# The first expert's threshold search: eight of fourteen rounds behind a branch

## The chip, the core and the metric

The kernel runs on one core of a Trainium2 chip. Its engines are TensorE (PE, matmuls; PEld are its weight loads), VectorE (DVE), ScalarE (ACT), GpSimd (POOL) and SyncE (SP, which here issues DMAs); each works off its own queue of instructions in order, and they wait for each other by semaphores. The metric is the device time of one execution in microseconds.

## What is computed

Attention over blocks, and behind it a mixture of eight experts whose tokens are chosen greedily. Cut to what matters:

```python
def _moe_ref(x, w_gate, w1, w2):        # x: 4608 tokens x 512, from the attention
    logits = x @ w_gate                 # 4608 x 8
    order = np.argsort(-logits.flatten())
    for idx in order:                   # best (token, expert) pairs first
        tok, e = idx // 8, idx % 8
        if assigned[tok] >= 0 or counts[e] >= 576: continue
        assigned[tok] = e; counts[e] += 1
    for e in range(8):
        out[assigned == e] = np.maximum(x[assigned == e] @ w1[e], 0) @ w2[e]
```

The kernel does not sort. It asks which expert is filled first: each token proposes its best open expert, and the expert whose 576th proposal is the highest takes its 576 tokens. Then tokens and expert are struck out and the same is done for the next.

## The kernel before

Up to about 315 us the attention runs; its last step gives the logits `L`. The second stage routes and computes eight experts. `route(k)` finds expert k and its tokens, `gather` fetches them by an indirect DMA of GpSimd, `weights` fetches the expert's weights by SyncE and splits them into two fp16 halves, and `ffn` does the two matmuls (`h`, then `y`). For k from 1 on `route` runs beside the `ffn` of an earlier expert. For k = 0 nothing runs beside it: there are no tokens yet.

`route` holds the proposals twice, as `PV` (a token's logits on one partition) and as `PB` (transposed, so that each group of partitions holds one expert). The search finds the 576th proposal of all experts at once. Each of `NS` = 14 rounds cuts the interval to a quarter: it places three borders in it (`cd`, `bs`), counts the proposals above each (two counts `jk` on VectorE, line 761 or 762, one count `ja` on ScalarE, line 735, by an accumulated sign), sums the counts over partitions by a small matmul (`tot`, line 782), and derives by how many quarters the lower border `lo` moves (`sg`, line 785). At round `NSC` = 6 the proposals are shifted by the border reached (`P2`, line 739), so that the later, smaller steps keep their precision.

After the last round lines 789 to 827 choose: two additions and three small transposes bring border and width to every partition (`th`, `bc`), a maximum finds the expert, and a one-hot vector `oh` picks its borders (`los`, `lo2s`, `hi2s`) and its number `ei`. From these come a mask of the tokens above the interval (`MM[:,0]`) and of those at or above the lower border (`ge`); the difference is `MM[:,1]`, of which as many are taken as there is room for. `eidx` (line 824) is the expert's number, which SyncE loads into a register (line 926) before it fetches the weights. Scans (`SC`, line 831) and position matmuls (`po`, lines 843 to 850) number the tokens, `invert` makes the list `ix` (lines 884 to 913), eight matmuls `warm` (line 920) keep TensorE at work until the gather (`xg`, line 985) lands, and transposes (`xt`, line 1006) put the tokens in the layout of `h` (line 1040).

The order on the engines is made by a planner (`Sched`), when the program is built: the pieces are Python generators that yield engine and cost, and the planner takes the one that can start first. A queue holds instructions in the order in which it took them. `sc.busy`, `sc.lag` and the yielded costs are its estimates; what changes in them changes how later pieces are woven into each other.

Of the kernel before, what the change touches and what calls it, by code (L numbers as in the profile page):

```python
# [596 lines left out]
class Moe:  # L597
    def __init__(s,tc,nc,ctx,sc,L,xd,w1,w2,out):
        s.tc,s.nc,s.sc,s.L,s.xd,s.w1,s.w2,s.out=tc,nc,sc,L,xd,w1,w2,out
        s.NT=xd.shape[0]; s.D=w1.shape[1]; s.E=w1.shape[0]; s.F=w1.shape[2]; s.CAP=s.NT//s.E; s.C=s.NT//P  # L600
        s.NS=14; s.NSC=6
        s.cp=ctx.enter_context(tc.tile_pool(name="mcp",bufs=1))
        s.ident=s.cp.tile([P,P],F32,name="mident"); make_identity(nc,s.ident)
        s.am=s.cp.tile([P,8],F32,name="m_am"); s.nam=0; nc.gpsimd.memset(s.am,2.0**-50)
        s.ab=s.cp.tile([P,1],F32,name="m_ab")
        s.vm=s.cp.tile([P,s.C],F32,name="m_vm"); s.nP=s.cp.tile([P,s.C,s.E],F32,name="m_nP"); s.Lr=s.cp.tile([P,s.C,s.E],F32,name="m_Lr")
        N=s.C*s.E; s.PAD=s.CAP*s.E//P
        s.PB,s.P2=[s.cp.tile([P,N+s.PAD],F32,name=n) for n in ("m_PB","m_P2")]
# [86 lines left out]
    def route(s,k):  # L695
# [19 lines left out]
        else:  # L715
# [29 lines left out]
            for t in range(s.NS):  # L745
                w=4.0**-t
                cnt=rp.tile([P,3],F16,tag="cnt",name=f"cn{k}_{t}")
                cand=base
                if t:
                    cand=rp.tile([P,3],F32,tag="cand",name=f"cd{k}_{t}")  # L750
                    yield D,s.CD[0 if k==0 else 1 if k<3 else 2],('P2',k) if PBx is not PB else None
                    if k==0: V.tensor_tensor(cand[:,2:3],base[:,2:3],nw,op=OP.add)
                    else:
                        for i in (2,0,1): V.tensor_scalar(cand[:,i:i+1],lo,nw,(i+1)*w,op0=OP.add,op1=OP.add)
                P2=s.P2 if t==s.NSC else None
                sc.add(signs(PBx,cand[:,2:3],cnt,t,P2),s.PR['signs'],sc.now+200)
                sc.nolat()
                for i in range(2):
                    yield D,429
                    jk=rp.tile([P,N],F16,tag="jk",name=f"jk{k}_{t}_{i}")  # L760
                    if t and k==0: V.scalar_tensor_tensor(jk,base[:,i:i+1].to_broadcast([P,N]),nw,PBx[:,:N],op0=OP.add,op1=OP.is_gt,accum_out=cnt[:,i:i+1])  # L761
                    else: V.tensor_scalar(jk,PBx[:,:N],cand[:,i:i+1],0.0,op0=OP.is_lt,op1=OP.add,accum_out=cnt[:,i:i+1])
                    if i==0: sc.nolat()
                if k==0 and t==3:
                    dg=rp.tile([32,1024],F16,name="m_dg",bufs=1)
                    nc.gpsimd.indirect_dma_start(out=dg,out_offset=None,in_=s.xd,in_offset=bass.IndirectOffsetOnAxis(ap=s.it[:32,P-1:P],axis=0))
                add=lambda o,a,b: V.tensor_tensor(o,a,b,op=OP.add) if k==0 else V.tensor_scalar(o,a,b,None,op0=OP.add)
                if t: add(lo,lo,nw)
                if P2 is not None:
                    V.tensor_scalar(CB[:,2:3],lo,-1.0,None,op0=OP.mult); sc.set(('nlo',k))  # L770
                    lo=CB[:,1:2]; PBx=P2
                if t==s.NS-1: add(CB[:,2:3],CB[:,0:1],lo)
                elif k==0:
                    base=rp.tile([P,3],F32,tag="base",name=f"bs{k}_{t}")
                    V.tensor_scalar(base,s.io3g,w/4,lo,op0=OP.mult,op1=OP.add)
                    if t==1:
                        V.reciprocal(s.g[:,2:3],s.g[:,1:2])
                        nc.gpsimd.tensor_scalar(fl(Lm),fl(s.L),s.g[:,2:3],None,op0=OP.mult)
                sc.busy(D,330 if k==0 else 150)
                yield T,30,('sg',k,t)  # L780
                tot=s.ps.tile([P,512],F32,tag="tot",name=f"tot{k}_{t}")
                nc.tensor.matmul(tot[:,0:3],lhsT=s.bo,rhs=cnt,start=True,stop=True)  # L782
                yield D,72
                sg=rp.tile([P,4],F32,tag="sg",name=f"sg{k}_{t}")
                V.scalar_tensor_tensor(sg[:,0:3],tot[:,:3],s.NT-s.CAP+0.5,(wk[:,t:t+1]).to_broadcast([P,3]),op0=OP.is_le,op1=OP.mult,accum_out=sg[:,3:4])
                nw=sg[:,3:4]
                sc.lag(s.XG if k>2 and t<s.XT else s.LG)
            yield D,140
            V.tensor_scalar(CB[:,2:3],CB[:,2:3],nw,None,op0=OP.add)
            V.tensor_scalar(lo,lo,nw,None,op0=OP.add)  # L790
            yield T,90,'rt'
            tk=sc.take(); ps=s.ps.tile([P,512],F32,tag="rt",name=f"bc{k}")
            th=s.ps.tile([P,512],F32,tag="tot",name=f"th{k}")
            nc.tensor.transpose(th[:,:32],CB[:32,2:3].to_broadcast([32,P]),s.ident[:32,:32])
            for i in range(2): nc.tensor.transpose(ps[:,32*i:32*i+32],CB[:32,i:i+1].to_broadcast([32,P]),s.ident[:32,:32])
            BC=s.BC[k%2]; th=th[:,0:8]

            f=rp.tile([P,2,8],F32,tag="f",name=f"f{k}"); m1=rp.tile([P,6],F32,tag="m1",name=f"m1{k}")
            yield D,77
            V.tensor_reduce(m1[:,0:1],th,axis=AX.X,op=OP.max)  # L800
            yield D,138
            V.scalar_tensor_tensor(f[:,0],th,m1[:,0:1],s.wt8,op0=OP.is_equal,op1=OP.mult)
            V.tensor_copy(BC[:,0:2],ps[:,:64].rearrange("p (i x) -> p i x",i=2)[:,:,0:8])
            V.tensor_scalar(BC[:,2],ps[:,32:40],w if k else wk[:,s.NS-1:s.NS],None,op0=OP.add); sc.set(tk)
            yield D,77
            V.tensor_reduce(m1[:,1:2],f[:,0],axis=AX.X,op=OP.max)
            oh=f[:,1]
            yield D,133
            V.tensor_scalar(oh,f[:,0],m1[:,1:2],None,op0=OP.is_equal)
# [12 lines left out]
            ge=rp.tile([P,C],F16,tag="ge",name=f"ge{k}")
            V.tensor_scalar(ge,ds_,los,lo2s,op0=OP.subtract,op1=OP.is_ge)
            V.tensor_copy(eidx,ei)
            sc.add(s.weights(k,eidx),s.PR['weights'],sc.now)
            yield D,106
            V.tensor_tensor(MM[:,1],ge,MM[:,0],op=OP.subtract)
# [307 lines left out]
```

## Time and profile before

| | us |
|---|---|
| median of three runs | 765.41 |
| lowest, highest | 763.78, 765.56 |
| the profiled execution, time | 765.04 |
| the profiled execution, span from first to last instruction | 763.3 |
| busy in that span: TensorE, VectorE, ScalarE, GpSimd | 709.0, 561.3, 514.5, 380.5 |

The profile is of one execution. A row of the instructions in order of time gives the start and the duration in us, the engine, the line, the operation, and output <- input; in brackets stands how long the engine idled before and what ended it. Shares over the whole span say little here, since the two stages and the seam between them have different limits; rows of the seam, from 315 to 365 us, are what is read below.

### The profile page before, as it was taken

Reading aid. Unit: us, or ns where it says so; the run is one execution under the profiler, and the core shown is the slowest. Engines: PE = TensorE matmul, PEld = TensorE weight load, DVE = VectorE, ACT = ScalarE, POOL = GpSimd, SP = SyncE. Lnnn points to the kernel's source line nnn. Section 1 sums busy time; section 2 is a strip of 40 time slices with the busy share of each in tenths; the row PEclk is TensorE's granted clock in tenths of the full one; section 3 lists DMA queues with packets and bytes.
Section 4 is the critical chain, followed back from the end, with each engine's and each line's share of the span. In section 5 each row is a group of like instructions: output and inputs, shape, how many; then the busy total and the mean of one; then the engine's idle time right before and its main releaser. Section 6 shows DMA issues by size and latency. Waiting matters only on the chain.

```text
span 763.3 us, 18351 instructions
## 1 busy us (share of the span) xinstructions
PE 709.0 (93%) x6321; PEld 456.9 (60%) x6321; DVE 561.3 (74%) x2293; ACT 514.5 (67%) x1395; POOL 380.5 (50%) x455
## 2 busy tenths in 40 slices
PE   5999999999999999417999999999989999999997
PEld 3666776666666766305546747657556475574753
DVE  6999989798979979887989978869678596020210
ACT  4887889878787777335838778594964956583211
POOL 6876563636655652203414457293670843796001
PEclk9999999999999999856999999999999999999999
DMA  9899999999999998608027075591963916992001
GB/s 194 163 204 192 213 206 186 230 177 232 185 229 187 220 201 166 186 4 280 6 109 230 8 259 149 169 220 41 256 133 135 239 36 222 211 282 70 32 15 48
DMA packets 273517, 124.48 MB, mean 163 GB/s; under 512 B 247296, under 2 KB 256512, under 8 KB 273424
## 3 DMA queue, kind: packets, MB, share of 16 engines
q1 hardware_dynamic: 267504, 104.37, 63.2%
q0 software_dynamic: 5920, 18.95, 8.2%
q8 instruction: 49, 0.80, 0.5%
q14 instruction: 44, 0.36, 0.2%
HBM read 71.39 MB, written 18.87 MB: 118 GB/s over the span
## 4 chain that ended last, share of the span: by engine, by line
PE 49%; issue 4%; DMA 2%; DVE 2%; ACT 1%; POOL 1%; POOLq 0%; DVEq 0%; ACTq 0%
PE h L1040 25%; PE y L1066 19%; PE y L1070 3%; DMA raw<-in_moe_w_dram 1%; PE pe L901 1%; DMA xg<-x,ix 1%; DVE jk L761 1%; POOL xg L985 1%; PE xt L1006 0%; PE tot L782 0%; PE psb L487 0%; DMA out_dram<-yo,ix 0%; PE psb L437 0%; ACT ja L735 0%; POOL W L948 0%
## 5 line engine op out<-in xcount | busy, mean ns | idle before, releaser
L1040 PE MATMUL h<-X,W 128*128 128x320 f16 (+3 forms) x1536 | 195.2, 287 | 0.6 <-DVE HL L1028 0.5
L393 ACT ACTIVATE P<-psb,m 128x576 f32<-128x576 f32 (+8 forms) x288 | 149.6, 548 | 38.5 <-DVE m L389 35.4
L1040 PEld LDWEIGHTS <-W 128*128 128x128 f16 x1536 | 142.9, 98 | 42.5 <-issue 3.0
L948 POOL TENSOR_TENSOR W<-raw,W 128x1024 f16<-128x1024 f32 x56 | 118.4, 2137 | 80.2 <-ACT W L946 79.7
L1066 PE MATMUL y<-W,HH 128*128 128x512 f16 x512 | 152.4, 379 | 0.0
L385 DVE TENSOR_REDUCE m<-psb 128x1 f32<-128x576 f32 (+8 forms) x288 | 124.5, 479 | 11.4 <-PE psb L367 10.7
L437 PE MATMUL psb<-mident,P 128*128 128x128 f32 x800 | 105.6, 279 | 4.8 <-DVE Xf L454 1.7
L437 PEld LDWEIGHTS psb<-mident,P 128*128 128x128 f32 x800 | 85.8, 141 | 23.4 <-ACT P L393 6.6
L1026 ACT ACTIVATE HH<-h 128x320 f16<-128x320 f32 (+3 forms) x128 | 51.8, 411 | 68.9 <-PE h L1040 67.4
L1066 PE MATMUL y<-W,HL 128*128 128x512 f16 x256 | 97.1, 379 | 0.0
L487 PE MATMUL psb<-PT,V 128*64 128x448 f32 (+5 forms) x776 | 96.7, 390 | 0.2 <-ACT PT L418 0.2
L1056 POOL DMA_INDIRECT out_dram<-yo,ix x40 | 39.1, 977 | 114.3 <-ACT yo L1048 78.7
L367 PE MATMUL psb<-kT,qT 128*64 128x512 f16 (+7 forms) x640 | 86.6, 294 | 3.1 <-ACT P L393 1.3
L367 PEld LDWEIGHTS <-qT 128*64 128x64 f16 x1280 | 61.4, 111 | 38.8 <-issue 17.7
L418 ACT ACTIVATE PT<-psb 128x512 f32<-128x512 f32 (+1 forms) x157 | 79.3, 580 | 7.4 <-PE psb L437 5.5
L1028 DVE SCALAR_TENSOR_TENSOR HL<-h,HH 128x320 f16<-128x320 f32 (+3 forms) x128 | 57.3, 452 | 36.2 <-ACT HH L1026 35.7
L367 PE MATMUL psb<-kS,qT 128*64 128x512 f16 (+7 forms) x640 | 78.9, 289 | 0.0
L1066 PEld LDWEIGHTS <-HH 128*128 128x128 f16 x512 | 46.5, 98 | 53.3 <-issue 2.6
L942 ACT ACTIVATE raw<-raw 128x512 f32<-128x512 f32 x112 | 67.5, 625 | 11.2 <-DMA raw<-in_moe_w_dram 11.2
L487 PEld LDWEIGHTS psb<-PT,V 128*64 128x64 f32 x776 | 48.6, 138 | 34.9 <-issue 24.4
L946 ACT ACTIVATE W<-raw 128x512 f16<-128x512 f32 x112 | 67.7, 625 | 0.0
L393 ACT ACTIVATION_READ_ACCUMULATOR P<-psb,m 128x1 f32 x288 | 65.1, 226 | 0.0
(230 smaller groups left out, 1034.5 us busy)
## 6 DMA issues: line engine op xcount, KB each, us to landing
raw<-in_moe_w_dram SPq DMA_DIRECT2D x64, 512.0 KB, 5.7
x<-XR SPq DMA_DIRECT2D x8, 1152.0 KB, 6.9
kn<-in_k_dram SPq DMA_DIRECT2D x15, 576.0 KB, 6.1
qn<-in_q_dram SPq DMA_DIRECT2D x15, 576.0 KB, 8.1
V<-in_v_dram SPq DMA_DIRECT2D x64, 128.0 KB, 2.9
V<-in_v_dram SPq DMA_DIRECT2D x16, 64.0 KB, 2.9
xg<-x,ix POOLq DMA_INDIRECT x40, 4.6
out_dram<-yo,ix POOLq DMA_INDIRECT x40, 2.9
```

Source lines behind the costliest of these rows:

```text
L367: nc.tensor.matmul(ps[64 * h:64 * h + 64, o + a:o + e], lhsT=A[:, h, 64 * i:64 * i + 64], rhs=K[:, h, a:e], start=st, stop=not st)
L385: nc.vector.tensor_reduce(m[:, 0, c:c + 1], ps[:, o:o + 64 * (i + 1)], axis=AX.X, op=OP.max)
L393: nc.scalar.activation(Pt[:, s.OFF[i]:s.OFF[i] + 64 * (i + 1)], ps[:, o:o + 64 * (i + 1)], AF.Exp, bias=m[:, 1, c:c + 1], scale=s.ESC, acc ...
L418: s.nc.scalar.activation(out, in_, AF.Copy)
L437: nc.tensor.transpose(ps[:, a], s.Pb[n % s.NP][:, s.OFF[i] + 128 * j:s.OFF[i] + 128 * j + P], s.ident)
L487: nc.tensor.matmul(ps[64 * h:64 * h + 64, 64 * (i0 - b0):64 * (b1 - b0)], lhsT=vn[:, j, 2 * (n % 2) + h, :], rhs=pt[:, s.PTI[(j, i0)]:s.PT ...
L942: nc.scalar.activation(raw[:,x],raw[:,x],AF.Copy,scale=s.WS)
L946: nc.scalar.activation(hi[:,x],raw[:,x],AF.Copy)
L948: nc.gpsimd.tensor_tensor(lw,raw,hi,op=OP.subtract)
L1028: nc.vector.scalar_tensor_tensor(HL[:,f,ts],ps,0.0,HH[:,f,ts],op0=OP.max,op1=OP.subtract)
L1040: nc.tensor.matmul(ps,lhsT=W[:,a,d,f*P:f*P+P],rhs=X[:,4*(d//2)+d%2+l,ts],start=(d==0 and n==0),stop=(d==3 and n==2))
L1066: if m<4: nc.tensor.matmul(ps,lhsT=Z[:,f,m*P:m*P+P],rhs=Y[:,a,f],start=(f==n==0),stop=(f==7 and n==2))
```

## The change

Only the first search changes. It runs six rounds and chooses at once. A flag `bi` says whether that choice may stand: it is 0 if one expert alone has the highest border (the sum of `f` equals its maximum) and if exactly 576 of its logits are at or above the lower border (`cg`, summed by a matmul with ones). VectorE, TensorE and ScalarE load the flag into a register, and the block with rounds 7 to 14 and a second choice is jumped over when it is 0. `eidx` moves behind that block. The rounds and the choice become inner functions, and for the block they are built without the planner; behind it the planner is told that three engines were busy 1500 ns.

```diff
-        s.NS=14; s.NSC=6
+        s.NS=14; s.NSC=6; s.TB=6
...
-            for t in range(s.NS):
-                w=4.0**-t
...
+            def rounds(t0,t1):
+                nonlocal lo,nw,PBx,base
+                for t in range(t0,t1):
+                    w=s.wlast=4.0**-t
...
+                    if t<s.TB or k: sc.add(sg_,s.PR['signs'],sc.now+200)
+                    else:
+                        next(sg_); next(sg_,0)
...
+                    if t and (k or t!=s.TB): add(lo,lo,nw)
...
+            def choose(t1,n,guess):
...
+                V.scalar_tensor_tensor(f[:,0],th,m1[:,0:1],s.wt8,op0=OP.is_equal,op1=OP.mult,**(dict(accum_out=m1[:,6:7]) if guess else {}))
...
+                V.tensor_scalar(MM[:,0],ds_,los,hi2s,op0=OP.subtract,op1=OP.is_gt)
+                if guess:
+                    with nc.allow_low_precision(reason="whole numbers up to 36"):
+                        V.tensor_scalar(ge,ds_,los,lo2s,op0=OP.subtract,op1=OP.is_ge)
+                        V.tensor_reduce(cg[:,0:1],ge,axis=AX.X,op=OP.add)
+                else: V.tensor_scalar(ge,ds_,los,lo2s,op0=OP.subtract,op1=OP.is_ge)
+                if k: load()
+                yield D,106
+                V.tensor_tensor(MM[:,1],ge,MM[:,0],op=OP.subtract)
...
+            if k:
+                yield from rounds(0,s.NS)
+                yield D,140
+                end()
+                yield from choose(s.NS,1,False)
+            else:
...
+                yield from rounds(0,s.TB)
+                yield D,140
+                V.tensor_tensor(CB[:,2:3],lo,nw,op=OP.add)
+                V.tensor_tensor(lo,lo,nw,op=OP.add)
+                yield from choose(s.TB,1,True)
+                yield T,100
+                tot=s.ps.tile([P,512],F32,tag="tot",name="m_ct")
+                nc.tensor.matmul(tot[:,0:1],lhsT=s.ones,rhs=cg,start=True,stop=True)
+                yield D,150
+                V.tensor_tensor(bad[:,0:1],m1[:,6:7],m1[:,1:2],op=OP.not_equal)
+                V.scalar_tensor_tensor(bi,tot[:,0:1],float(s.CAP),bad[:,0:1],op0=OP.not_equal,op1=OP.max)
+                ET=mybir.EngineType
+                rv=nc.values_load(bi[0:1,0:1],engines=(ET.DVE,ET.PE,ET.Activation),min_val=0,max_val=1)
+                with s.tc.If(rv>0):
+                    for x in rounds(s.TB,s.NS): pass
+                    end()
+                    for x in choose(s.NS,0,False): pass
+                for x in (D,T,A): sc.busy(x,1500)
+                yield D,150
+                load()
```

VectorE's queue behind the sixth round's decision (`sg_5`), before: the next round follows, and far below `eidx` stands between the mask `ge` and its difference.

```order
L785 SCALAR_TENSOR_TENSOR sg_5_5040<-tot_5_5038,m_wkg 128x3
L752 TENSOR_TENSOR cd_6_5043<-bs_5_5036,sg_5_5040 128x1
L761 SCALAR_TENSOR_TENSOR jk_6_0_5046,cn_6_5042<-bs_5_5036,sg_5_5040,m_PB 128x288
...
L823 TENSOR_SCALAR ge_5195<-ds_5188,m_5179 128x36
L824 CAST eidx_4943<-m_5179 128x1
L827 TENSOR_TENSOR MM_4941<-ge_5195,MM_4941 128x36
L831 SCALAR_TENSOR_TENSOR SC_4942<-m_ones,MM_4941 128x36 x2
```

Now the choice follows at once, then the count, the flag, its load and the jump; 64 rows further on the block ends, and `eidx` and the scan stand behind it.

```order
L800 SCALAR_TENSOR_TENSOR sg_5_5050<-tot_5_5048,m_wkg 128x3
L853 TENSOR_TENSOR m_CB_84<-m_CB_84,sg_5_5050 128x1
...
L835 TENSOR_REDUCE m_cg<-ge_4951 128x1
L839 TENSOR_TENSOR MM_4941<-ge_4951,MM_4941 128x36
L860 TENSOR_TENSOR m_bad<-m_4946 128x1
L861 SCALAR_TENSOR_TENSOR m_bi<-m_ct,m_bad 128x1
L863 TENSOR_LOAD m_bi
L864 COMPARE_AND_BRANCH
...
L864 UNCONDITIONAL_BRANCH x2
L752 CAST eidx_4943<-m_4946 128x1
L874 SCALAR_TENSOR_TENSOR SC_4942<-m_ones,MM_4941 128x36 x2
```

The choice moved ahead of round 7, and `eidx` behind the end of the block. SyncE's and GpSimd's queues hold what they held, in the same order, with one jump more.

TensorE's queue in the first `ffn`, before: the second search's matmul of round 0 (`tot_0`), all of `h_4` and `h_5`, then that of round 1 (`tot_1`).

```order
L782 MATMUL tot_0_5480<-cn_0_5438,m_bo 128x3
L1040 LDWEIGHTS W_0_5207
L1040 MATMUL h_4_0_5491<-X_5306,W_0_5207 128x128
...
L1040 MATMUL h_5_0_5515<-X_5306,W_0_5207 128x128
L782 LDWEIGHTS m_bo
L782 MATMUL tot_1_5532<-cn_1_5485,m_bo 128x3
```

Now `tot_1` stands ahead of them, behind the last three matmuls each of `h_2` and `h_3`.

```order
L797 MATMUL tot_0_5518<-cn_0_5482,m_bo 128x3
L1083 LDWEIGHTS W_0_5247
L1083 MATMUL h_2_0_5416<-X_5345,W_0_5247 128x128
...
L1083 MATMUL h_3_0_5420<-X_5345,W_0_5247 128x128
L797 LDWEIGHTS m_bo
L797 MATMUL tot_1_5548<-cn_1_5529,m_bo 128x3
L1083 LDWEIGHTS W_0_5247
L1083 MATMUL h_4_0_5551<-X_5345,W_0_5247 128x128
```

Twenty-four matmuls moved behind `tot_1`. VectorE's queue at the same place, before: two evacuations (`HL`) stand between the decision and the next candidates.

```order
L785 SCALAR_TENSOR_TENSOR sg_0_5483<-tot_0_5480,m_wk 128x3
L1028 SCALAR_TENSOR_TENSOR HL_5363<-h_0_0_5366,HH_5362 128x128
L1028 SCALAR_TENSOR_TENSOR HL_5363<-h_1_0_5370,HH_5362 128x128
L754 TENSOR_SCALAR cd_1_5486<-CB_5422,sg_0_5483 128x1 x3
L762 TENSOR_SCALAR jk_1_0_5503,cn_1_5485<-m_PB,cd_1_5486 128x288
```

Now they stand behind the counts.

```order
L800 SCALAR_TENSOR_TENSOR sg_0_5527<-tot_0_5518,m_wk 128x3
L765 TENSOR_SCALAR cd_1_5530<-CB_5458,sg_0_5527 128x1 x3
L776 TENSOR_SCALAR jk_1_0_5538,cn_1_5529<-m_PB,cd_1_5530 128x288
L776 TENSOR_SCALAR jk_1_1_5541,cn_1_5529<-m_PB,cd_1_5530 128x288
L781 TENSOR_SCALAR CB_5458<-CB_5458,sg_0_5527 128x1
L1071 SCALAR_TENSOR_TENSOR HL_5396<-h_0_0_5405,HH_5395 128x128
```

Similar shifts follow up to the first `y`; from there on the rows are those of before.

## Rows read from the trace of the kernel before

**Rows 1.** Busy windows: stretch, length, each engine's busy time, granted clock, DMA share, GB/s.

```profile
320.00:330.00 10.00, 1.12 (x6) 0.62 (x6) 8.75 (x56) 4.50 (x13) 1.10 (x1) 0.50 0.23 75
330.00:340.00 10.00, 1.83 (x10) 1.14 (x11) 8.86 (x59) 3.30 (x10) 0.00 (x0) 0.50 0.00 0
```

**Rows 2.** Instructions in order of time: end of the sixth and of the last round.

```profile
325.11 0.08 DVE L785 DVE_READ_ACCUMULATOR sg<-tot,m_wkg 128x1 f32 x1
...
337.92 0.08 DVE L761 DVE_READ_ACCUMULATOR jk<-bs,sg,m_P 128x1 f16 x1
...
338.07 0.19 PE L782 MATMUL tot<-cn,m_bo 128*128 128x3 f16 x1 [1.41 <-DVE jk L761]
...
338.29 0.16 DVE L785 SCALAR_TENSOR_TENSOR sg<-tot,m_wkg 128x3 f32<-128x3 f32 x1
338.38 0.08 DVE L785 DVE_READ_ACCUMULATOR sg<-tot,m_wkg 128x1 f32 x1
```

**Rows 3.** Instructions in order of time: the choice, the mask and the scan.

```profile
339.81 0.24 PE L843 MATMUL po<-m_sh,m_ones 128*128 128x72 f16 x1 [0.53 <-DVE m L806]
...
341.42 0.30 DVE L823 TENSOR_SCALAR ge<-ds,m 128x36 f16<-128x36 f32 x1
341.63 0.15 DVE L824 CAST eidx<-m 128x1 int32<-128x1 f32 x1
...
341.85 0.35 DVE L831 TENSOR_TENSOR_SCAN SC<-m_ones,MM 128x36 f16<-128x36 f16 x2
```

**Rows 4.** Instructions in order of time: the first gather and the first transposes.

```profile
347.67 0.99 POOL L985 DMA_INDIRECT xg<-x,ix  x1 [23.20 <-issue]
...
352.50 1.04 PE L1006 MATMUL xt<-m_idh,xg 128*128 128x128 f16 x8 [2.42 <-DMA xg<-x,ix]
```

**Rows 5.** Busy windows of the later stage.

```profile
380.00:400.00 20.00, 20.00 (x142) 9.11 (x141) 16.79 (x87) 7.08 (x16) 1.98 (x2) 1.00 0.24 90
...
520.00:560.00 40.00, 38.09 (x279) 22.52 (x278) 27.61 (x144) 26.84 (x63) 21.51 (x15) 1.00 0.69 174
```

**Rows 6.** Line 926 on SyncE: nanoseconds min/median/max; all eight, then the first alone.

```profile
L926 SPq TENSOR_LOAD <-eidx x8: 268/282/485, 342.0 to 639.1; - x8
L926 SPq FUSED_REGOPS  x8: 152/160/187, 342.5 to 639.5; - x8
L926 SPq SEQ_ASSERT  x8: 18/18/33, 342.8 to 639.7; - x8
...
L926 SPq TENSOR_LOAD <-eidx x1: 485/485/485, 342.0 to 342.0; - x1
```

**Rows 7.** Busy windows (columns as in rows 1): DMA after the attention's last writes.

```profile
322.00:323.00 1.00, 0.00 (x0) 0.00 (x0) 0.90 (x5) 0.64 (x2) 0.00 (x0) 0.50 0.00 1
```

**Rows 8.** Instructions in order of time: dummy gather, warming, first FFN beside second search.

```profile
323.37 1.10 POOL L766 DMA_INDIRECT m_dg<-x,m_it  x1 [3.65 <-DVE m_CB L767]
...
346.49 3.59 PE L920 MATMUL warm<-OL,m_ones 128*128 128x512 f16 x8
...
354.60 0.85 PE L1040 MATMUL h<-X,W 128*128 128x128 f16 x6
...
361.01 0.48 DVE L1028 SCALAR_TENSOR_TENSOR HL<-h,HH 128x128 f16<-128x128 f32 x2
...
361.35 1.50 PE L1040 MATMUL h<-X,W 128*128 128x128 f16 x24 [0.49 <-DVE HL L1028]
...
362.54 0.21 ACT L735 ACTIVATION_READ_ACCUMULATOR ja<-m_PB,cd 128x1 f16 x1
...
362.80 0.17 PE L782 MATMUL tot<-cn,m_bo 128*128 128x3 f16 x1
...
363.11 2.07 PE L1040 MATMUL h<-X,W 128*128 128x128 f16 x27
```

**Rows 9.** DMA issues of the dummy gather: count, us from issue to landing.

```profile
m_dg<-x,m_it POOLq DMA_INDIRECT x1, 2.7
```

**Rows 10.** Busy windows: granted clock (third number from the right) at its return.

```profile
358.00:358.10 0.10, 0.10 (x5) 0.10 (x3) 0.00 (x0) 0.06 (x1) 0.00 (x0) 0.86 1.16 451
```

More of the change, by code (lines that the diff above doesn't have):

```diff
@@ L744, in route @@
             lo=CB[:,0:1]; nw=s.zero; PBx=PB; wk=s.wk if k else s.wkg
-            for t in range(s.NS):
-                w=4.0**-t
[L747 to L809, printed above, removed]
+            f=rp.tile([P,2,8],F32,tag="f",name=f"f{k}"); m1=rp.tile([P,8],F32,tag="m1",name=f"m1{k}"); oh=f[:,1]
             sm=rp.tile([P,4,8],F32,tag="sm",name=f"sm{k}")
             d2=R("d2"); ds_=rp.tile([P,C],F32,tag="ds",name=f"ds{k}")
-            yield D,463,'pp'
-            V.tensor_tensor(sm,BC,oh[:,None,:].to_broadcast([P,4,8]),op=OP.mult)
@@ L814, in route @@
-            V.tensor_tensor(d2,PV,be(oh),op=OP.mult)
-            yield D,670
-            V.tensor_reduce(m1[:,2:6],sm,axis=AX.X,op=OP.add)
             los,lo2s,hi2s,ei=[m1[:,i:i+1] for i in range(2,6)]
-            V.tensor_reduce(ds_,d2,axis=AX.X,op=OP.add)
             u=rp.tile([P,8],F32,tag="u8",name=f"u8{k}")
-            yield D,540 if k>2 else 420
-            V.tensor_scalar(MM[:,0],ds_,los,hi2s,op0=OP.subtract,op1=OP.is_gt)
             ge=rp.tile([P,C],F16,tag="ge",name=f"ge{k}")
-            V.tensor_scalar(ge,ds_,los,lo2s,op0=OP.subtract,op1=OP.is_ge)
@@ L824, in route, with load @@
[L824 to L827, printed above, removed]
+            def load():
+                V.tensor_copy(eidx,ei)
+                sc.add(s.weights(k,eidx),s.PR['weights'],sc.now)
+            def rounds(t0,t1):
+                nonlocal lo,nw,PBx,base
+                for t in range(t0,t1):
+                    w=s.wlast=4.0**-t
+                    cnt=rp.tile([P,3],F16,tag="cnt",name=f"cn{k}_{t}")
+                    cand=base
+                    if t:
+                        cand=rp.tile([P,3],F32,tag="cand",name=f"cd{k}_{t}")
+                        yield D,s.CD[0 if k==0 else 1 if k<3 else 2],('P2',k) if PBx is not PB else None
+                        if k==0: V.tensor_tensor(cand[:,2:3],base[:,2:3],nw,op=OP.add)
+                        else:
+                            for i in (2,0,1): V.tensor_scalar(cand[:,i:i+1],lo,nw,(i+1)*w,op0=OP.add,op1=OP.add)
+                    P2=s.P2 if t==s.NSC else None
+                    sg_=signs(PBx,cand[:,2:3],cnt,t,P2)
+                    if t<s.TB or k: sc.add(sg_,s.PR['signs'],sc.now+200)
+                    else:
+                        next(sg_); next(sg_,0)
+                    sc.nolat()
+                    for i in range(2):
+                        yield D,429
+                        jk=rp.tile([P,N],F16,tag="jk",name=f"jk{k}_{t}_{i}")
+                        if t and k==0: V.scalar_tensor_tensor(jk,base[:,i:i+1].to_broadcast([P,N]),nw,PBx[:,:N],op0=OP.add,op1=OP.is_gt,accum_out=cnt[:,i:i+1])
+                        else: V.tensor_scalar(jk,PBx[:,:N],cand[:,i:i+1],0.0,op0=OP.is_lt,op1=OP.add,accum_out=cnt[:,i:i+1])
+                        if i==0: sc.nolat()
+                    if k==0 and t==3:
+                        dg=rp.tile([32,1024],F16,name="m_dg",bufs=1)
+                        nc.gpsimd.indirect_dma_start(out=dg,out_offset=None,in_=s.xd,in_offset=bass.IndirectOffsetOnAxis(ap=s.it[:32,P-1:P],axis=0))
+                    add=lambda o,a,b: V.tensor_tensor(o,a,b,op=OP.add) if k==0 else V.tensor_scalar(o,a,b,None,op0=OP.add)
+                    if t and (k or t!=s.TB): add(lo,lo,nw)
+                    if P2 is not None:
+                        V.tensor_scalar(CB[:,2:3],lo,-1.0,None,op0=OP.mult); sc.set(('nlo',k))
+                        if k==0: next(sg_,0)
+                        lo=CB[:,1:2]; PBx=P2
+                    if t==s.NS-1: add(CB[:,2:3],CB[:,0:1],lo)
+                    elif k==0:
+                        base=rp.tile([P,3],F32,tag="base",name=f"bs{k}_{t}")
+                        V.tensor_scalar(base,s.io3g,w/4,lo,op0=OP.mult,op1=OP.add)
+                        if t==1:
+                            V.reciprocal(s.g[:,2:3],s.g[:,1:2])
+                            nc.gpsimd.tensor_scalar(fl(Lm),fl(s.L),s.g[:,2:3],None,op0=OP.mult)
+                    if k or t<s.TB: sc.busy(D,330 if k==0 else 150)
+                    yield T,30,('sg',k,t)
+                    tot=s.ps.tile([P,512],F32,tag="tot",name=f"tot{k}_{t}")
+                    nc.tensor.matmul(tot[:,0:3],lhsT=s.bo,rhs=cnt,start=True,stop=True)
+                    yield D,72
+                    sg=rp.tile([P,4],F32,tag="sg",name=f"sg{k}_{t}")
+                    V.scalar_tensor_tensor(sg[:,0:3],tot[:,:3],s.NT-s.CAP+0.5,(wk[:,t:t+1]).to_broadcast([P,3]),op0=OP.is_le,op1=OP.mult,accum_out=sg[:,3:4])
+                    nw=sg[:,3:4]
+                    if k or t<s.TB: sc.lag(s.XG if k>2 and t<s.XT else s.LG)
@@ new lines, in end @@
+            def end():
+                V.tensor_scalar(CB[:,2:3],CB[:,2:3],nw,None,op0=OP.add)
+                V.tensor_scalar(lo,lo,nw,None,op0=OP.add)
+            if k:
[3 more added lines that the diff above has]
+                yield from choose(s.NS,1,False)
+            else:
+                cg=rp.tile([P,1],F16,name="m_cg",bufs=1); bad=rp.tile([P,2],F32,name="m_bad",bufs=1); bi=rp.tile([P,1],I32,name="m_bi",bufs=1)
+                yield from rounds(0,s.TB)
[18 more added lines that the diff above has]
+                load()
@@ L974 @@
     ML,SL,ST,WT=100,0,500,200
-    PR=dict(route=0,weights=1,gather=2,ffn=2,hev=2,yev=0,signs=0,conv=4,out=0)
+    PR=dict(route=0,weights=1,gather=2,ffn=2,hev=2,yev=0,signs=0,conv=4,conv0=0,out=0)
     WS=32.0; XS=64.0; NWU=8; NWM=0; GW=1; GS=2
```

26 lines of the change are left out of this document (added).

## The prediction

> **What bounds the kernel now.** I read the busy windows first [rows 1]. From 320 to 340 us TensorE is busy 1.12 and 1.83 us of each 10, DMA all but stops, and VectorE is busy 8.8 of 10: one chain of small VectorE steps holds the whole core. The instructions in order of time show which [rows 2]. It is the first expert's search: a round is candidate, two counts, ScalarE's count beside them, a small matmul and a decision, each waiting for the one ahead. The sixth round's decision is read out at 325.11 + 0.08 = 325.19, the fourteenth's at 338.38 + 0.08 = 338.46. Then the choice of the expert follows, the scan of the mask, the list of tokens and the first gather [rows 3, 4], all in series; the first transposes of gathered tokens stand at 352.50. From there TensorE is the bound: full in 380 to 400, and short by 1.91 us in 520 to 560 [rows 5]. So a microsecond taken from the chain before 352.5 moves all that follows forward, unless the work at the seam between the two stages changes.
>
> **Part 1, what goes.** Rounds 7 to 14, and with them the wait between 6 and 7: 338.46 - 325.19 = **13.27 us** of pure chain (1.66 a round), if the jump is taken. Whether it is depends on the data alone. The condition: after six rounds one expert alone has the highest threshold, and exactly 576 (4608/8) of its logits lie at or above the lower border. I worked the search through on the reference's own inputs: one expert leads after four rounds already (0.344 of the scale; the next has 0.281), and the count at or above its border is 576 after four, five, six and fourteen rounds. After six, 575 of them lie above the whole interval. The result does not hang on a rounding.
>
> **Part 2, what comes on the path.** The choice itself (transposes, maximum, one-hot, the sums, the mask) was on the path before and only moves: from 338.46 to the end of the mask `ge`, 341.42 + 0.30 = 341.72, 3.26 us [rows 2, 3]. Moved by 13.27 its end is 328.45. New, between there and the scan:
> - the sum of `ge` over 36 columns: a step of its size, 0.15 to 0.20 us by the `eidx` and decision rows; 0.20;
> - the counting matmul: in a search round the counts end at 337.92 + 0.08 = 338.00, the matmul starts at 338.07 and takes 0.19 [rows 2]; 0.25. It is at the lower clock there, as before;
> - `bi`, by the decision it resembles: starts 0.03 after the matmul's end and takes 0.16; 0.19. `bad` and the other half of the mask run under the matmul and cost nothing; without that cover 0.15 each;
> - the load of the flag into a register on three engines in parallel. SyncE does the same with `eidx` [rows 6]: 0.22 us from its write (341.78) to the load at 342.0, then 0.27 to 0.485 for the load, 0.16 and 0.02 for the register steps. 0.70 to 0.90; 0.80;
> - two jumps on each engine and a semaphore addition. No row shows a jump. Low end: three sequencer steps like the 18 ns assertion, 0.05; high end: each jump as dear as a median register load, 0.60. I take 0.30, between, since register steps of 0.16 are nearest in kind;
> - `eidx` now stands ahead of the scan with nothing between, 0.12 to the scan by the steps around it.
> The sum is 1.86; with the ends of load and jump 1.51 to 2.26. The scan starts at 328.45 + 1.86 = 330.31 instead of 341.85 [rows 3]: **11.54 us** earlier, 11.14 to 11.89.
>
> [...]
>
> What the new wait holds up: behind the load on VectorE stand `eidx` and the scan, on TensorE the position matmuls, on ScalarE the scaling of the one-hot, needed 2 us later. The first two position matmuls stood ahead of the scan before (the first at 339.81 [rows 3]); now they start with the jump and must end before the scan does, 0.35 us later: 0 to 0.2 us, I take **0.1**. The load also waits for every DMA that SyncE has issued so far and for GpSimd's steps. At 328.9 that is over: DMA share is 0.00 in 322 to 323, and GpSimd's last step, a dummy gather, is issued by 324.5 and has even landed 2.7 us later [rows 7 to 9]. If that cover were gone, its rest would be added whole. SyncE and GpSimd get one jump each, after their last DMA of that stage; they idle there and are needed only for the weights and the gather.
>
> Weights and gather both start from the scan's neighbourhood, as before, so the 10.2 us from scan to first transposes stay.
>
> **Part 3, the order at the seam.** The planner saw other times, so the first FFN and the second search are woven differently. On TensorE the matmul of the second search's round 1 (`tot_1`) stood behind 24 matmuls of `h_4` and `h_5`; now it stands ahead of them, behind 6. Its counts come late: ScalarE's are read out at 362.54 + 0.21 = 362.75, and `tot_1` goes at 362.80 [rows 8]. Before, the 24 matmuls ran in that gap (1.50 us from 361.35) and `h_6` followed at 363.11. Now they start behind `tot_1`: at 362.85 if it stays where it is, so they end at 364.35, and `h_6` is 1.24 us late. Against that, VectorE goes from `sg_0` straight to the candidates, ahead of two evacuations (0.48 us), and ScalarE counts before it copies the last token tile, so `tot_1` is ready earlier. I take the 0.48 once: 1.24 - 0.48 = **0.8 us lost**; 0.3 if both save as much, 1.3 if neither does. From there TensorE was unbroken before, and from the first `y` on the order is that of before, so it isn't won back; the 1.91 us idle at 520 to 560 could take some in.
>
> **Part 4, the clock.** The granted clock is 0.50, the lower level, all through the search [rows 1] and returns to full at 358.0 to 358.1, 3.45 us after the first `h` matmul at 354.60 [rows 8, 10]. The activity that brings it back is shifted as a whole. Nothing shows that the return shifts by just as much: the eight warming matmuls, 3.59 us from 346.49 [rows 8], did not bring it in before. If it takes twice as long from the first `h`, 3.45 us more pass at half speed, and up to 1.7 us are lost; if it comes 0.6 us sooner, 0.3 are won. I take 0.3 lost.
>
> **Sum.** 11.54 - 0.1 - 0.8 - 0.3 = 10.3 us. The profiled execution took 765.04 (span 763.3): 754.7. It lies 0.4 under the median of the three runs; halfway to that, the forecast is **754.9 us**. Its own bounds: best 11.89 + 0.3 - 0.3 = 11.9 and a start at the lowest run, 763.78, give 751.9, with all extremes at once; worst 11.14 - 0.2 - 1.3 - 1.7 = 7.9 give 757.1.
>
> **Rivals.**
> (a) The jump costs a fetch of instructions. On VectorE some 64 rows are skipped. If the target has to be brought from memory, all three engines stand until it lands. The page lists instruction queues with packets of 16 KB, but no row times one; the nearest are the landings of 2.7 us for the dummy gather and 4.8 for the first real gather (347.67 to 352.50) [rows 4, 9]. That gives 754.9 + 2.7 to 4.8 = 757.6 to 759.7, say **758.6**. For it: nothing in this kernel jumped until now. Against it: 64 rows are few beside VectorE's whole stream, which is fetched as it runs, and in the chain of before nothing stands still for that long. [...]
> (b) The jump is not taken, since on the chip the sixth round leaves two experts or a count other than 576. Then the 13.27 us stay, and the first choice, check and load come on top: 3.26 + 1.86 - 0.12 = 5.0, with the seam 0.8: 765.0 + 5.8 = **770.8**, slower. It decides from one logit between the border and the 576th. Against it stands the count above, with margin from the fourth round on.
> (c) The gain is earned and lost again: TensorE, bound from 354 on, meets a wait on weights or on a later search that was hidden. The price is another one like the 1.91 us of 520 to 560 [rows 5], and the seam at its upper end, 0.5 more: 754.9 + 2.4 = **757.3**.
>
> **How the numbers follow.** Forecast 0.77, (a) 0.11, (b) 0.04, (c) 0.08. The range must leave out no more than 0.2: from 752.6 (the extremes of the low end do not come together) to 758.4, which takes in (c) and the near part of (a). A measurement of this kernel tells 0.3%, 2.3 us, from no change. All cases but (b) are faster by more: 0.95; within 0.3% 0.01; slower 0.04.
>
> **What would show it.** Right: in the profile after, six pairs of counts with `k` 0, then the choice, a register load of 0.3 to 0.5 us on VectorE, TensorE and ScalarE, no row of a seventh round between; the scan starts near 330.3 and the first transposes near 341. At the seam TensorE waits 1 to 2 us on ScalarE's count at `tot_1`. Wrong: a gap of over 2 us between the load and `eidx` (a); two choices (b); transposes at 341 but an end later than 757 (c or the clock).

## Result and the profile after

The changed kernel takes **754.38 us** (median of four runs, 753.41 to 756.14) against 765.48 before: ratio 0.9862, 95% interval 0.9839 to 0.9885. The profiled execution is the fastest, 753.41 us, with a span of 751.6 us against 763.3. In the chain of instructions in order of time (answers to [rows 2 to 4]; start, duration, engine, line, operation, in brackets the idle time before):

```profile
324.54 0.08 DVE L800 DVE_READ_ACCUMULATOR sg<-tot,m_wkg 128x1 f32 x1
...
327.54 0.30 DVE L834 TENSOR_SCALAR ge<-ds,m 128x36 f16<-128x36 f32 x1
327.87 0.19 DVE L835 TENSOR_REDUCE m_cg<-ge 128x1 f16<-128x36 f16 x1
...
328.12 0.18 PE L858 MATMUL m_ct<-m_cg,m_ones 128*128 128x1 f16 x1 [2.64 <-DVE m_cg L835]
328.34 0.16 DVE L861 SCALAR_TENSOR_TENSOR m_bi<-m_ct,m_bad 128x1 int32<-128x1 f32 x1
...
330.14 0.15 DVE L752 CAST eidx<-m 128x1 int32<-128x1 f32 x1 [1.63 <-DVEq L864]
330.21 0.35 DVE L874 TENSOR_TENSOR_SCAN SC<-m_ones,MM 128x36 f16<-128x36 f16 x2
...
335.99 0.98 POOL L1028 DMA_INDIRECT xg<-x,ix  x1 [12.00 <-DMA raw<-in_moe_w_dram]
...
341.50 0.62 PE L1049 MATMUL xt<-m_idh,xg 128*128 128x128 f16 x8 [3.08 <-DMA xg<-x,ix]
```

No row of a seventh round stands between. Set against before, stretch by stretch:

| stretch | before | after | difference |
|---|---|---|---|
| start to end of the sixth round | 325.19 | 324.62 | -0.57 |
| sixth round's end to the scan | 16.66 | 5.59 | -11.07 |
| scan to first transposes | 10.65 | 11.29 | +0.64 |
| first transposes to first `y` | 30.44 | 30.59 | +0.15 |
| first `y` to the end | 380.31 | 379.54 | -0.77 |
| span | 763.25 | 751.63 | -11.62 |

The second line is the change. The first lies ahead of it; whether the last three belong to it is what the experiments have to say. Where the new 2.37 us between mask and scan are is told by the flag's load and the branch, each on three engines (nanoseconds, then first and last start):

```profile
L863 DVEq EVENT_SEMAPHORE  x5: 49/50/50, 328.4 to 328.8; - x5
L863 ACTq TENSOR_LOAD <-m_bi x1: 462/462/462, 328.7 to 328.7; - x1
L863 PEldq TENSOR_LOAD <-m_bi x1: 486/486/486, 328.7 to 328.7; - x1
L863 DVEq TENSOR_LOAD <-m_bi x1: 542/542/542, 328.9 to 328.9; - x1
L863 DVEq FUSED_REGOPS  x1: 222/222/222, 329.5 to 329.5; - x1
L863 DVEq SEQ_ASSERT  x1: 35/35/35, 329.7 to 329.7; - x1
```

```profile
L864 ACTq COMPARE_BRANCH  x1: 50/50/50, 329.2 to 329.2; - x1
L864 PEldq COMPARE_BRANCH  x1: 219/219/219, 329.3 to 329.3; - x1
...
L864 DVEq COMPARE_BRANCH  x1: 72/72/72, 329.8 to 329.8; - x1
L864 DVEq EVENT_SEMAPHORE  x1: 21/21/21, 330.0 to 330.0; - x1
```

VectorE's load is the longest and starts last, so it sets the end: five steps of 0.05 us, 0.10 from start to start, for the semaphores, 0.54 for the load, 0.26 for register and assertion, 0.07 for the branch. At the seam (answer to [rows 8]) TensorE now waits:

```profile
348.78 0.16 PE L797 MATMUL tot<-cn,m_bo 128*128 128x3 f16 x1
...
350.48 0.24 ACT L735 ACTIVATION_READ_ACCUMULATOR ja<-m_PB,cd 128x1 f16 x1
...
350.78 0.16 PE L797 MATMUL tot<-cn,m_bo 128*128 128x3 f16 x1 [1.48 <-ACT ja L735]
350.88 2.34 PE L1083 MATMUL h<-X,W 128*128 128x128 f16 x39
```

The busy windows (columns of [rows 1]) show the clock's return, 4.4 us behind the first transposes and not 5.55 [rows 10], and that the wait of [rows 5] between 520 and 560 is gone:

```profile
520.00:560.00 40.00, 40.00 (x304) 23.73 (x303) 29.09 (x156) 31.30 (x74) 24.50 (x17) 1.00 0.70 192
...
345.80:345.90 0.10, 0.10 (x4) 0.10 (x2) 0.10 (x1) 0.10 (x1) 0.00 (x0) 0.59 1.16 451
345.90:346.00 0.10, 0.10 (x5) 0.10 (x3) 0.10 (x1) 0.03 (x1) 0.00 (x0) 1.00 0.94 369
```

### The profile page after: what moved, and what is told of

It reads as the page before. It is cut to its first block, busy times and chain, and to the rows that moved or that the text cites. A ratio compares the mean times of both kernels' runs of the same rounds, so it can differ in the third digit from the quotient of the medians.

```text
span 751.6 us, 18263 instructions
## 1 busy us (share of the span) xinstructions
PE 705.6 (94%) x6314; PEld 455.0 (61%) x6314; DVE 550.6 (73%) x2224; ACT 508.7 (68%) x1378; POOL 380.3 (51%) x455
## 4 chain that ended last, share of the span: by engine, by line
PE 47%; DMA 3%; issue 3%; ACT 2%; POOL 1%; DVE 1%; SPq 0%; POOLq 0%; ACTq 0%
PE h L1083 24%; PE y L1109 18%; PE y L1113 3%; DMA raw<-in_moe_w_dram 2%; DMA xg<-x,ix 1%; PE pe L944 1%; POOL xg L1028 1%; ACT ja L735 0%; DMA out_dram<-yo,ix 0%; PE xt L1049 0%; PE tot L797 0%; SPq L1006 0%; ACT raw L985 0%; POOL W L991 0%; POOL out_dram L1099 0%
```

## Experiments

Every kernel was timed beside the kernel before. In the three groups of runs that took 770.3, 766.5 and 764.2 us, so only ratios are compared. An interval is 3 to 6 us wide, more than most effects here, so the stretches decide. In the table, all in us: search start to scan, end of the (first) mask to scan, scan to first transposes, first transposes to first `y`, and how long after the first transposes the granted clock was back at 1.00 for good.

| kernel | ratio, interval | search | mask to scan | gather | to `y` | clock |
|---|---|---|---|---|---|---|
| before | 1 | 26.52 | 0.13 | 10.65 | 30.44 | 5.6 |
| after | 0.9862, 0.9839-0.9885 | 15.45 | 2.37 | 11.29 | 30.59 | 4.4 |
| e_after_again | 0.9858, 0.9833-0.9883 | 15.45 | 2.36 | 10.95 | 30.69 | 4.7 |
| e_no_check | 0.9845, 0.9810-0.9880 | 13.37 | 0.28 | 11.38 | 30.30 | 3.8 |
| e_load_only | 0.9879, 0.9838-0.9920 | 15.14 | 2.05 | 10.85 | 30.84 | 4.6 |
| e_far_jump | 0.9890, 0.9864-0.9917 | 18.30 | 5.21 | 11.06 | 31.16 | 5.3 |
| e_mid_jump | 0.9896, 0.9875-0.9917 | 18.15 | 5.05 | 10.79 | 31.28 | 5.6 |
| e_forced | 1.0065, 1.0034-1.0096 | 31.57 | 18.48 | 11.09 | 30.70 | 4.4 |
| e_order_before | 0.9852, 0.9818-0.9886 | 15.44 | 2.36 | 11.84 | 30.80 | 5.4 |
| e_order_exact | 0.9862, 0.9836-0.9887 | 15.45 | 2.36 | 10.96 | 30.30 | 5.3 |
| e_before_neworder | 1.0005, 0.9987-1.0024 | 26.54 | 0.12 | 10.73 | 30.87 | 5.0 |
| e_tb4 | 0.9803, 0.9768-0.9838 | 12.62 | 2.72 | 11.96 | 30.27 | 3.6 |
| e_tb4_order | 0.9821, 0.9793-0.9850 | 12.62 | 2.72 | 10.93 | 30.64 | 5.1 |
| e_tb4_exact | 0.9803, 0.9776-0.9831 | 12.75 | 2.73 | 10.81 | 30.53 | 5.8 |

The search column repeats to 0.02 us wherever it should, which no other column does; the one exception is e_tb4_exact, where a single row, the mask `ge`, took 0.43 us instead of 0.30.

### The same kernel once more

> The changed kernel once more, for a second profile of it. Theory: 754.4 us; the first gather lands 5.5 us after its issue as in the first profile of it (4.8 in the profile before), since it starts 12 us sooner, among SyncE's loads of the weights. Rival: the 0.64 us between the scan and the first transposes are the spread of one transfer, and a second profile shows 4.8 to 5.2 us.

```profile
337.08 0.99 POOL L1028 DMA_INDIRECT xg<-x,ix  x1 [10.86 <-DMA raw<-in_moe_w_dram]
...
342.23 0.62 PE L1049 MATMUL xt<-m_idh,xg 128*128 128x128 f16 x8 [2.72 <-DMA xg<-x,ix]
```

The gather took 337.08 to 342.23 = 5.15 us here, 5.51 in the first profile, 4.83 before; over the kernels with the early gather the stretch from the scan spreads from 10.79 to 11.96. Half of the 0.64 us is gone at once, and the column's spread is twice its size, so the expectation of 5.5 us fails and the 0.64 is not shown to belong to the change. A part of it may: all twelve kernels with the early choice lie above the two without (10.65 and 10.73), by 0.5 on average, and why is open. From the first `y` on this profile has 380.58 us, 0.3 more than before. So the 0.8 us less is spread as well, and the wait lost between 520 and 560 bought nothing that can be shown.

### What the check costs

```diff
-                nc.tensor.matmul(tot[:,0:1],lhsT=s.ones,rhs=cg,start=True,stop=True)
...
-                rv=nc.values_load(bi[0:1,0:1],engines=(ET.DVE,ET.PE,ET.Activation),min_val=0,max_val=1)
-                with s.tc.If(rv>0):
-                    for x in rounds(s.TB,s.NS): pass
-                    end()
-                    for x in choose(s.NS,0,False): pass
```

All of it but the sum of `ge`, which nothing reads any more, is left out in e_no_check; in e_load_only the flag and its load stay, and the last four lines go.

> The changed kernel with the check left out: six rounds, the choice, and then straight on; no count matmul, no flag, no register load, no branch, and no rounds 7 to 14 behind one, so the kernel would be wrong on an input that six rounds don't settle. Each queue behind it is in the changed kernel's order. Theory: the profile after has 2.37 us from the end of the mask to the scan (327.84 to 330.21), the one before 0.13; so the check costs 2.24 us, and this kernel takes 752.1 us, with the scan 2.2 us sooner after the sixth round's end than in the changed kernel (about 3.4 us instead of 5.6). Rival: the load hides something that is late anyway (GpSimd, the position matmuls), and at least half of that comes back as a wait before the first transposes: 753.3 us or more.

> The changed kernel with flag and register load on three engines, but nothing behind them: the two jumps and the block with rounds 7 to 14 are left out. Same order on each queue behind it. Theory: in the profile after the compare-and-branch takes 50 to 219 ns and stands 0.3 us ahead of eidx on VectorE, so this kernel is 0.3 us faster than the changed one, 754.1 us; the load with its semaphore and register steps stays at 1.2 to 1.4 us from the flag's end to eidx. Rival: the jumps are what makes the step long (1.64 us from the flag's end to eidx, where 1.10 was forecast), through the fetch of instructions behind them: then the step falls to 0.8 us and the time to 753.5 us.

Without the check the scan comes 15.45 - 13.37 = 2.08 us sooner, not 2.24; without branch and block 0.31. What is missing is the sum, which stayed: e_no_check still has 0.28 us between mask and scan, where 0.13 stood before. So the whole check is 2.2 us. Whether some of it comes back as a wait before the first transposes is not settled: the gather's 11.38 us lie within that column's spread. The sum in e_no_check, then the flag and `eidx` in e_load_only, instructions in order of time:

```profile
326.98 0.19 DVE L835 TENSOR_REDUCE m_cg<-ge 128x1 f16<-128x36 f16 x1
```


```profile
329.90 0.16 DVE L861 SCALAR_TENSOR_TENSOR m_bi<-m_ct,m_bad 128x1 int32<-128x1 f32 x1
331.37 0.15 DVE L752 CAST eidx<-m 128x1 int32<-128x1 f32 x1 [1.31 <-issue]
```

From the end of the flag, 330.06, to `eidx` 1.31 us remain of the 1.64 after: the load is 1.31, the branch 0.33. The rival that put the long step on the jump (a fall to 0.8) falls. The ratios can't tell 2.1 or 0.3 us.

### Where the jump goes

```diff
                     for x in choose(s.NS,0,False): pass
+                    for x in range(600): V.tensor_copy(bad[:,1:2],bad[:,0:1])
```

None of these runs; e_mid_jump has 200. The block itself is 93 rows of VectorE, counted where it runs (e_forced), with the reads of accumulators and the semaphore steps that the 64 of the list ahead leave out. So the target lies some 90, 290 and 690 away in the changed kernel, e_mid_jump and e_far_jump.

> The changed kernel with 600 one-column copies more on VectorE at the end of the block that is jumped over; none of them runs. [...] Rival: the distance of the target doesn't matter, 754.4 us and 0.1 to 0.3 us from the branch to eidx as in the changed kernel.

> The changed kernel with 200 one-column copies more at the end of the skipped block on VectorE, where 600 of them kept VectorE standing for 2.9 us between branch and target; the target is now some 270 instructions away. None of the copies runs. [...]

Line 864 of e_far_jump, then of e_mid_jump:

```profile
L864 DVEq COMPARE_BRANCH  x1: 72/72/72, 329.5 to 329.5; - x1
L864 DVEq EVENT_SEMAPHORE  x1: 21/21/21, 332.5 to 332.5; - x1
```

```profile
L864 DVEq COMPARE_BRANCH  x1: 72/72/72, 328.9 to 328.9; - x1
L864 DVEq EVENT_SEMAPHORE  x1: 21/21/21, 331.8 to 331.8; - x1
```

VectorE stands for 2.8 to 3.0 us between the branch and the next step, where the changed kernel shows 0.1 to 0.2, so the distance does matter. In the windows of e_far_jump, with DMA idle otherwise, 8 GB/s pass in one microsecond of that gap, 8 KB; in its DMA queues the second instruction queue has 46 packets where the changed kernel has 44:

```profile
329.60:330.60 1.00, 0.00 (x0) 0.00 (x0) 0.00 (x0) 0.00 (x0) 0.00 (x0) 0.50 0.00 0
330.60:331.60 1.00, 0.00 (x0) 0.00 (x0) 0.00 (x0) 0.00 (x0) 0.00 (x0) 0.50 0.02 8
```

```profile
q14 instruction: 46, 0.38, 0.2%
```

That fits rival (a), which was only not met: the block is short enough. Its price, put at 2.7 to 4.8 us, is 2.70 to 2.85 by the search column. With 290 rows VectorE stands about as long as with 690, and e_mid_jump too has 8 KB in one microsecond of the gap and 46 packets. In the kernel before, 44 packets of 8 KB go with 5639 rows of VectorE, ScalarE, GpSimd and SyncE (semaphore and register steps included), an estimated 128 rows to a packet, and by that both targets lie beyond the next packet. A jump that ends in the next packet was not tried, and the limit is only known to lie between 90 and 290.

### The branch not taken

```diff
-                with s.tc.If(rv>0):
+                with s.tc.If(rv<1):
```

> The changed kernel with the branch's condition turned round: the flag is 0, and the block with rounds 7 to 14 and the second choice runs although it isn't needed. It is what an input costs that six rounds don't settle. Theory: the rival (b) of the prediction with the check as measured (2.37 us instead of 1.98): 13.27 us for the rounds and 3.26 us for the second choice on top of the changed kernel, 754.4 + 16.5 = 770.9 us. Rival: the block's order isn't planned (ScalarE's count is queued at once with its round) and its rounds take less or more than 1.66 us; at 1.5 us 769.6 us, at 1.8 us 772.0 us.

```profile
329.17 0.16 DVE L861 SCALAR_TENSOR_TENSOR m_bi<-m_ct,m_bad 128x1 int32<-128x1 f32 x1
...
332.13 0.08 DVE L800 DVE_READ_ACCUMULATOR sg<-tot,m_wkg 128x1 f32 x1
...
343.27 0.08 DVE L800 DVE_READ_ACCUMULATOR sg<-tot,m_wkg 128x1 f32 x1
...
347.15 0.35 DVE L874 TENSOR_TENSOR_SCAN SC<-m_ones,MM 128x36 f16<-128x36 f16 x2
```

The scan comes 31.57 - 15.45 = 16.1 us later than with the jump, and 5.05 later than before: rival (b) said 5.0. The ratio gives 765.48 x 1.0065 = 770.5 us for its 770.8. The rounds in the block take (343.27 - 332.13) / 7 = 1.59 us. Before, the eight took 13.27; 8 x 1.59 leaves 0.55, of which 0.46 was one idle stretch of VectorE between rounds 6 and 7, some 0.35 longer than that between other rounds.

### The order at the seam

```diff
-                sc.add(s.weights(k,eidx),s.PR['weights'],sc.now)
+                sc.add(s.weights(k,eidx),s.PR['weights'],sc.now-(200 if k==0 else 0))
```

This gives the changed kernel the order of before behind the token list (e_order_exact); 212 added instead gives the kernel before the changed order (e_before_neworder). Another edit, e_order_before, reaches that order but for VectorE's weight splits:

```diff
                 load()
+                sc.busy(D,800)
```

Its first `h` came 2.9 us behind the first transposes instead of 1.9, so it is inconclusive on the order.

> The changed kernel with the planner's time for the first expert's weights 200 ns earlier, so that behind the list of tokens every queue has exactly the order of the kernel before, VectorE too; nothing else differs. Theory: at an equal return of the clock the changed order costs TensorE 0.8 us between the first transposes and the first y. The profiles so far with the changed order show 30.27 us there when the clock is back 3.5 us behind the first transposes and 31.16 when it takes 5.3, half a microsecond for each; so this kernel shows 0.8 us less than that line (29.9 at 4.5 us, 30.4 at 5.4), no wait at tot_1, and takes 753.7 us against 754.4. Rival: the order costs nothing there, and the stretch lies on the line of the changed order, 30.3 to 31.2.

> The kernel before with all 14 rounds and no branch, and the planner's time for the first expert's weights 212 ns later, so that behind the list of tokens every queue has exactly the order of the changed kernel. Theory: 0.8 us slower than the kernel before, 766.2 us, with 31.2 us from the first transposes to the first y if the clock is back 5.4 us behind them, and a wait of TensorE of 1.5 us at tot_1. Rival: the same time as before, 765.5 us, and 30.4 us there.

> The changed kernel, with the planner told of 800 ns more on VectorE behind the load of the first expert's number; from the list of tokens on TensorE, ScalarE, GpSimd and SyncE then have the order of the kernel before, and VectorE but for two splits of weights. Theory: the order at the seam costs 0.75 us (from the first transposes to the first y the profile after has 30.59 us and before 30.44, though the clock came back 0.6 us sooner with respect to the transposes); 753.6 us, with no wait of TensorE for ScalarE's count at tot_1. Rival: what the seam loses is won back later, since the 1.9 us wait in the stretch 520 to 560 went away with it (0.85 us less from the first y to the end); then this kernel has that wait again and takes 754.4 us or more.

First transposes, the second search's round 1 and first `y`, of e_order_exact and of e_before_neworder:

```profile
341.45 0.82 PE L1049 MATMUL xt<-m_idh,xg 128*128 128x128 f16 x6 [2.72 <-DMA xg<-x,ix]
...
351.63 0.16 PE L797 MATMUL tot<-cn,m_bo 128*128 128x3 f16 x1
...
371.75 0.59 PE L1109 MATMUL y<-W,HH 128*128 128x512 f16 x2
```

```profile
353.21 0.62 PE L1006 MATMUL xt<-m_idh,xg 128*128 128x128 f16 x8 [2.49 <-DMA xg<-x,ix]
...
362.77 0.16 PE L782 MATMUL tot<-cn,m_bo 128*128 128x3 f16 x1 [1.49 <-ACT ja L735]
...
384.08 0.59 PE L1066 MATMUL y<-W,HH 128*128 128x512 f16 x2
```

The wait at `tot_1` goes with the order, in either kernel. To weigh it, the clock must be held equal, since it came back anywhere from 3.6 to 5.8 us behind the first transposes, and a microsecond at half speed costs half a microsecond: with the changed order the stretch rises from 30.27 at 3.6 to 31.28 at 5.6. At 5.3 us the changed order shows 31.16 (e_far_jump) and the order of before 30.30 (e_order_exact); at 5.6, 31.28 (e_mid_jump) and 30.44 (before). That is 0.84 to 0.86 us. Within their windows the returns lie 0.1 us apart in each pair (5.32 against 5.24, 5.61 against 5.53), which is worth 0.04 to 0.05. **The order costs 0.8 us**, and in whole times that drowns: e_order_exact has the ratio of the changed kernel, e_before_neworder that of before. In the profiled executions the clock hid part of the 0.8, with 5.3 against 4.4 and 5.0 against 5.6.

### Four rounds

```diff
-        s.NS=14; s.NSC=6; s.TB=6
+        s.NS=14; s.NSC=6; s.TB=4
```

This alone is e_tb4; e_tb4_order has the 800 ns of e_order_before as well, e_tb4_exact the 200 ns of e_order_exact.

> The changed kernel with four rounds instead of six ahead of the choice; ten rounds in the block. Each queue behind it is in the same order. On these inputs four rounds leave one expert and a count of 576, so the block is jumped over. Theory: the search is a pure chain of 1.6 to 1.66 us a round and each round taken away counts whole: 3.25 us faster than the changed kernel, 751.1 us. Rival: the chain is no longer what is late, since the dummy gather issued in round 3 and GpSimd's steps now run into the register load (0.5 to 2.7 us of it): 752 to 754 us.

> Four rounds ahead of the choice, and 800 ns more told to the planner on VectorE, so that the first FFN and the second search are woven as in the kernel before. Theory: the two add up, 3.25 us for the rounds and 0.75 us for the order: 750.4 us. Rival: one of the two is taken back by a later wait, 751.1 us or more.

> Four rounds ahead of the choice, and the planner's time for the first expert's weights 200 ns earlier, so that behind the list of tokens every queue has exactly the order of the kernel before. Theory: 3.2 us for two rounds, less the 0.36 us that VectorE stood longer in the register load in both profiles with four rounds, and 0.8 us for the order: 3.6 us less than the changed kernel, 750.8 us. Rival: the order gives nothing, 751.5 us.

The scan comes 2.70 to 2.83 us sooner than with six rounds, not 3.2: mask to scan takes 0.36 longer in all three. Line 863 of e_tb4 shows where, VectorE's five semaphore steps (the other two engines pass theirs as quickly as before):

```profile
L863 PEldq EVENT_SEMAPHORE  x5: 51/51/120, 326.6 to 327.0; - x5
L863 DVEq EVENT_SEMAPHORE  x5: 49/50/50, 326.8 to 327.5; - x5
```

They span 0.7 us instead of 0.4. The dummy gather is not the cause: it was issued at 325.43 in e_tb4 and at 323.42 in e_tb4_order, and the hold is the same. The place is telling. Counted from the start of VectorE's rows, the hold stands ahead of row 1088 in all three kernels, and so does the idle stretch between rounds 6 and 7 in the kernel before; both are 0.35 us over the usual gap, and 0.7 to 0.9 us behind each 8 KB pass, in the kernel before as one packet of the second instruction queue. It goes with the place in the queue, then, and not with what stands there, which speaks for the step from one instruction packet to the next. With six rounds ahead of the choice no gap shows at that row, and no run moves it by itself, so this is argued and not shown. By the same count the branch of the changed kernel is row 1115 and the block behind it ends at row 1209 (e_forced). Both lie within 128 rows from 1088, so by the estimate the jump would stay inside one packet.

e_tb4_exact, with the order of before, and e_tb4, without it, share the **best ratio**, 0.9803, some 765.48 x 0.9803 = 750.4 us; both intervals lie below that of the changed kernel. So the 0.8 us of the order does not show in whole times here either. e_tb4_order, forecast at 750.4, has 751.8 by its ratio; its first `h` comes 2.9 us behind the first transposes, as in e_order_before. The gain rests on the inputs: four rounds settle them, as the prediction worked out.

## Why the prediction was right

754.9 us was forecast and 754.38 measured. By its steps:

- **Part 1** held: the jump is taken, and the 13.27 us are gone.
- **Part 2**, the choice: 3.22 us against 3.26. Sum of the mask, count matmul and flag: 327.84 to 328.50 = 0.66 against 0.20 + 0.25 + 0.19 = 0.64. The branch 0.33 against 0.30, with one row of a jump on each engine where two were counted. The scan's start behind `eidx` 0.07 against 0.12, and the position matmuls cost none of the 0.1: the second ends at 330.32, before the scan does.
- **The one mis-sized term is the register load**: 0.80 (0.70 to 0.90) was forecast, 1.31 measured. SyncE's rows [rows 6] were taken for VectorE's. There a load takes 0.28 in the median, here 0.54; a register step 0.16, here 0.22; and 0.22 us from the flag's write to the load became 0.35, since five semaphore steps stand between, each for two semaphores: those of eight DMA queues, of VectorE and of ScalarE; GpSimd's is the load's own. That they are long done saves the wait, not the steps. So the scan came 11.07 us earlier and missed the band of 11.14 to 11.89.
- **From scan to first transposes** nothing was to change (the 10.2 us named for it are 10.65 by [rows 3, 4]; the sum doesn't use them). 0.64 us were added in the first profile and 0.3 in the second, within the spread, of which the change may own some.
- **Part 3** held: the wait at `tot_1` was forecast at 1 to 2 us and is 1.48, and the order's cost was forecast at 0.8 and is 0.8. That it lands on the figure is partly luck, as 0.48 us were taken off once between bounds of 0.3 and 1.3.
- **Part 4** had the sign wrong in this execution: the clock came back about 1.2 us sooner behind the first transposes, which gave some 0.6 instead of taking 0.3. That is more than the 0.3 that the bounds allowed to be won; counted from the first `h`, as there, the return took 2.5 us and not 3.45. It is why the stretch shows only 0.15 us lost, and not 0.8.
- **Sum**: the load cost 0.5 more; the clock gave 0.9 more, and the stages outside the change 0.57 and 0.8, less 0.64 for the gather. Misses of both signs cancelled, so the closeness of the time is partly luck: the gain was forecast at 10.3 us and is 11.1 between the medians, 11.6 between the profiled executions. The scan's 330.21, where 330.31 was forecast, is luck too, since the rounds ahead of the change ended 0.57 earlier. By the chain alone, less the order, it is 11.07 - 0.8 = 10.3 us, as forecast.
- **Rivals**: (b) is right in size and did not occur; (a) did not occur at this distance; at 290 and 690 rows VectorE stands for 2.8 to 3.0 us, and what passes meanwhile is 8 KB, not a packet of the 16 KB that it names; (c) is not seen.

Open are whether the hold of 0.36 us is the step between two instruction packets, the exact distance at which a jump begins to wait, what part of the longer gather belongs to the change, and why the clock's return scatters by 2 us.

## What to carry to other kernels

Take the time of a serial chain from the rows, and price a branch on loaded data as sum, count, flag, load and jump in series: 2.2 us here, most of it the load on the slowest engine that must branch, with a step of 0.05 us (0.10 from start to start) for every two semaphores that it waits for. Keep what is jumped over short: on VectorE, where alone it was tried, the same jump over 290 instead of 90 rows costs 2.7 us more. Where an effect is below the spread of whole times, compare one stretch between two fixed instructions, and compare it at the same clock.

## What was not expected of the hardware

- A register load of one word from SBUF differs by engine: 0.28 us on SyncE (median), 0.46 on ScalarE, 0.49 on TensorE, 0.54 on VectorE; the compare with jump took 0.05, 0.22 and 0.07 on the last three.
- Behind the eight warming matmuls the clock did come back in the changed kernel, if not for long: the first eight transposes took 0.62 us there and 1.04 before, the clock was at 0.50 again 1 us behind their start, and full from 4.4 us on. In other executions of the same order (e_far_jump, e_mid_jump) it did not: it was at 0.50 there, and the first eight took 1.03 us. The windows of the changed kernel in which the clock rises and falls:

```profile
339.00:339.10 0.10, 0.00 (x0) 0.00 (x0) 0.10 (x1) 0.10 (x1) 0.10 (x1) 0.72 0.80 328
...
342.40:342.50 0.10, 0.00 (x0) 0.00 (x0) 0.10 (x2) 0.10 (x1) 0.10 (x1) 0.84 0.00 0
```
